# A fused attention and MLP kernel: one more batch turned by DMA, bursts keyed anew, and priorities drawn anew

## The chip, the cores and the metric

One core of one Trainium2 chip. The metric is the device time of one execution in microseconds (us), the median of several runs; lower is better.

## What is computed

Linear attention with random features, over 8 batches of 8 heads with 576 tokens each and 64 values per head, followed by an MLP over all 4608 tokens:

```python
def phi(x):
    proj = np.einsum('bhsd,md->bhsm', x, omega)
    h = proj - np.sum(x * x, axis=-1, keepdims=True) / 2.0
    h = h - np.max(h, axis=-1, keepdims=True)
    return np.exp(h) / np.sqrt(m)
kv = np.einsum('bhsm,bhsd->bhmd', k_p, v)
num = np.einsum('bhsm,bhmd->bhsd', q_p, kv)
den = np.einsum('bhsm,bhm->bhs', q_p, k_p.sum(axis=2))[..., None] + 1e-06
x = (num / den).transpose(0, 2, 1, 3).reshape(4608, 512)
h = x @ w_in                         # 512 -> 2048
g = h * np.clip(h + 3.0, 0.0, 6.0) / 6.0
out = g @ w_out                      # 2048 -> 512
```

with `q_p = phi(q * scale)` and `k_p = phi(k * scale)`.

## The kernel before

**A planner writes the order.** The kernel doesn't issue instructions as the Python runs. Each piece of work is declared with `op(engine, duration, emit, priority, reads, writes, ...)`, and `Prog.schedule` then runs a small model of the engines: it repeatedly takes, among the pieces that could start now on an engine, the one with the lowest priority value. The priorities are due times: one unit is one block of work (one batch of attention beside one block of the MLP). To them a table `NUDGE` adds some hundred small amounts, one per named piece. `Prog.emit` issues the pieces in the order found, engine by engine, with semaphores where one engine reads what another wrote. The order on each engine is fixed from then on; a piece that isn't ready holds back everything behind it on its engine, and on SP's queue every DMA behind it. PSUM is a ring of eight banks which the planner hands out.

**Attention, batch by batch** (`attention(b)`). k and q arrive from memory in bfloat16 by DMAs that GpSimd issues (from batch 1 on), v by DMAs that SP issues. 72 chunks of tokens by 64 values make 36 pairs, and two heads' chunks share a 128-row "double" (18 per batch). The steps of a batch:

- Turn k and q. For batches 0 to 2 TensorE transposes them into PSUM and DVE or ACT evacuates (`turns`); from batch 3 (`PE_T = 3`) SP issues DMA transposes.
- Project by omega. For batches 0 to 2 these are matmuls over 128 rows (pieces `K` and `Q`). From batch 3 (`ROWS = 3`) they are bursts of matmuls over 64 rows (pieces `R`, function `project_rows`, lines 736 and 739): for a range of doubles in `TU`, the two halves of the rows side by side, first all of k, then all of q. A burst takes two or four PSUM banks.
- ACT takes the exponential (pieces `eK`, `eQ`), DVE the maximum over the features (`mx`) and its reciprocal (`cc`).
- `pair(b, m)`, for each of four pairs of heads: v times the reciprocal (`vc`, on GpSimd or ACT, `vcl` on GpSimd), the product of k and v (`kv`, line 900), the numerator (`num`, line 929), the division (`div`, DVE line 945) into `xb`.
- Turn the output. For a batch below `PE_X = 3` (0, 1 and 2), `turn_x` does four TensorE transposes per pair (helper line 511) and one evacuation of 128x512 by DVE or ACT into `xT`; for the others SP issues one DMA transpose per pair (line 974). Block b of the MLP reads all of `xT` of batch b.

**MLP, block by block** (512 tokens of one batch; block 8 gathers the leftover 64 tokens of each batch). `mm1` multiplies by w_in (16 pieces of four matmuls of 512 columns, line 998), ACT takes a relu (line 1004), DVE the product with the capped half (line 1006) into `gT`. From block 1 on the second matrix product is done with seven products of quarters instead of eight (Strassen-Winograd): `products` issues pieces `P<block>.<n>` of 16 matmuls of 256 columns (line 1132), and the sums of quarters `S1` to `S4` (`combine`, line 1064, 16 per block of 128x512) run on GpSimd. Block 0 uses plain products (`mm2`, line 1048). The planner puts `products(blk - 1)` and `mm1(blk)` beside the attention of batch blk + 1.

The planner's durations that matter here:

```python
def combine(name, dst, x, y, minus, n, prio, reads, writes, engines=ADD):
    op(engines, {"POOL": 0.05 + n / 490.0, "DVE": 0.07 + n / 1920.0}, ...
```

Of the kernel before, what the change touches and what calls it, by code (L numbers as in the profile page):

```python
# [15 lines left out]
ROWS = 3  # L16
# [7 lines left out]
    ('Tevk0.11', 0): 0.0172, ('castq0.0A', 0): -0.0176, ('Tevq0.1A', 0): 0.1639, ('Tq0.1B', 0): -0.0037,  # L24
    ('Tevq0.1B', 0): 0.3021, ('Tk0.l', 0): 0.4022, ('Tevk0.l', 0): 0.0235, ('K0.0', 0): -0.1553,
    ('eK0.0', 0): -0.0153, ('K0.1', 0): 0.0442, ('eK0.1', 0): -0.0653, ('mx0.1', 0): -0.0395, ('eK0.2', 0): -0.042,
    ('K0.3', 0): 0.0766, ('K0.4', 0): 0.1229, ('eK0.4', 0): 0.2718, ('K0.5', 0): -0.0067, ('eK0.5', 0): 0.0177,
    ('K0.6', 0): -0.0736, ('eK0.6', 0): 0.1839, ('mx0.6', 0): 0.3237, ('K0.7', 0): -0.0092, ('eK0.7', 0): 0.8775,
    ('K0.8', 0): 0.0351, ('eK0.8', 0): 0.0218, ('mx0.8', 0): -0.0031, ('eQ0.0A', 1): 0.7881, ('vcl.0', 1): 0.0286,
    ('cc.0.0', 0): 0.1338, ('kvz.0.0', 0): 0.1537, ('num.0.0A', 0): 0.0042, ('rec.0.0A', 0): -0.0049,  # L30
    ('div.0.0A', 0): 0.0356, ('num.0.0B', 0): 0.0126, ('vc.0.1', 0): 0.4124, ('kv.0.1', 0): -0.0134,
    ('kvz.0.1', 0): 0.8635, ('num.0.1A', 0): 0.0126, ('rec.0.1A', 0): -0.009, ('div.0.1A', 0): 0.177,
    ('Xev.0.1A', 0): 0.6709, ('num.0.1B', 0): -0.0007, ('cc.0.2', 0): -0.0088, ('vc.0.2', 0): 0.1154,
    ('vcc.0.2', 0): -0.0808, ('num.0.2A', 0): 0.0126, ('rec.0.2A', 0): 0.08, ('vc.0.3', 0): -0.0114,
    ('vcc.0.3', 0): -0.0172, ('num.0.3A', 0): 0.7836, ('X.0.3B', 0): 0.0821, ('Xev.0.3B', 0): 0.0062,
    ('numL0', 0): -0.0033, ('divL0', 0): 0.0082, ('divL2', 0): 0.0082, ('k00.1', 0): 0.0095, ('kl.1', 0): -0.0088,
    ('ql0.1', 0): 0.0145, ('vl.1', 0): -0.119, ('v10.1', 0): -0.0099, ('Tevq1.2', 0): 0.0463, ('Tq1.4', 0): 0.7514,
    ('mx1.4', 0): -0.179, ('eK1.5', 0): 0.3592, ('mx1.5', 0): 0.3227, ('eK1.6', 0): 0.7632, ('mx1.7', 0): -0.561,
    ('mx1.8', 0): 0.0033, ('Q1.0', 1): 0.0073, ('eQ1.0', 1): 1.061, ('Q1.1', 0): 0.0184, ('Q1.1', 1): -0.0218,
    ('eQ1.1', 1): 0.9399, ('Q1.2', 1): 0.3729, ('eQ1.2', 1): -0.007, ('Q1.3', 0): 1.0729, ('vcl.1', 1): -0.0035,  # L40
    ('cc.1.0', 0): -0.1361, ('vc.1.0', 0): 0.0089, ('kv.1.0', 0): 0.0071, ('kvz.1.0', 0): -0.0003,
    ('rec.1.0A', 0): 0.0024, ('div.1.0A', 0): 0.0054, ('div.1.0B', 0): 0.0054, ('vc.1.1', 0): 0.0087,
    ('num.1.1A', 0): -0.002, ('div.1.1A', 0): 0.0054, ('div.1.1B', 0): 0.0054, ('Xev.1.1', 0): -0.0002,
    ('kv.1.2', 0): 0.9899, ('rec.1.2A', 0): -0.0101, ('div.1.2A', 0): 0.0075, ('div.1.2B', 0): 0.0054,
    ('X.1.2', 0): 0.0047, ('vc.1.3', 0): 0.6341, ('rec.1.3A', 0): -0.0016, ('div.1.3A', 0): 0.0054,
    ('div.1.3B', 0): 0.0054, ('mm1.0A.0p', 2): 0.0169, ('mm1.0A.2p', 1): 0.003, ('mm1.0A.2p', 2): 0.026,
    ('mm1.0A.4p', 2): 0.0282, ('mm1.0A.4', 0): 0.0113, ('relu.0A.4', 0): 0.1116, ('mm1.0A.6', 0): -0.0758,
    ('relu.0A.6', 0): -0.0575, ('mm1.0A.8', 0): -0.0075, ('g.0A.8', 0): -0.037, ('g.0A.10', 0): 0.0321,
    ('relu.0A.12', 0): 0.0317, ('mm1.0A.14', 0): 0.0222, ('relu.0B.12', 0): 0.7429, ('relu.0B.14', 0): 0.6881,
    ('k10.2', 0): -0.0002, ('kl.2', 0): -0.7114, ('q10.2', 0): 0.511, ('ql0.2', 0): 0.6465, ('Tevq2.3', 0): -0.6541,  # L50
    ('Tq2.4', 0): 1.2316, ('K2.2', 0): -0.7584, ('K2.5', 0): -0.3285, ('mx2.5', 0): -0.1483, ('K2.6', 0): 0.784,
    ('K2.7', 0): -0.0504, ('K2.8', 0): -0.1148, ('mm2.0.0', 3): -0.0049, ('mm2.0.0', 5): 1.9062,
    ('mm2.0.0', 6): 0.0051, ('mm2.0.1', 2): 0.0111, ('mm2.0.1', 5): 0.4836, ('mm2.0.2', 0): -0.0003,
    ('mm1.1.0', 0): -1.129, ('mm1.1.8', 0): -1.8251, ('g.1.8', 0): 0.0106, ('mm1.1.1', 0): -1.2275,
    ('mm1.1.9', 0): -0.9344, ('relu.1.9', 0): 0.0261, ('mm1.1.2', 0): -0.5674, ('mm1.1.10', 0): -1.3861,
    ('mm1.1.11', 0): -0.0435, ('mm1.1.4', 0): -0.3428, ('mm1.1.12', 0): 0.0488, ('mm1.1.13', 0): -0.1387,
    ('relu.1.13', 0): -0.4107, ('mm1.1.14', 0): 0.8048, ('mm1.1.7', 0): 0.8803, ('relu.1.7', 0): 0.0128,
    ('g.1.7', 0): -0.0389, ('mm1.1.15', 0): 1.161, ('k10.3', 0): -0.0369, ('kl.3', 0): 0.0052, ('q00.3', 0): -0.0024,
    ('q10.3', 0): 0.0694, ('ql0.3', 0): -0.0408, ('ql1.3', 0): -0.013, ('eK3.3.0', 0): 1.4387, ('R3.4', 0): -0.4628,
    ('eQ3.4', 0): -0.8607, ('kv.3.1', 0): 1.0065, ('vcc.3.2', 0): -0.4962, ('kv.3.2', 0): 0.1102,  # L60
    ('cc.3.3', 0): -0.8518, ('kvz.3.3', 0): 0.0243, ('P1.2', 0): 0.9757, ('P1.4', 0): 0.3487, ('P1.5', 1): -0.0512,
    ('P1.6', 1): 0.5369, ('mm1.2.0', 0): -1.4622, ('mm1.2.8', 0): -1.4018, ('mm1.2.1', 0): -1.442,
    ('g.2.1', 0): -0.019, ('mm1.2.9', 0): -0.3004, ('mm1.2.2', 0): -0.8136, ('mm1.2.11', 0): 0.359,
    ('mm1.2.12', 0): 0.5284, ('mm1.2.5', 0): 0.5493, ('mm1.2.6', 0): 0.5785, ('mm1.2.14', 0): 0.4337,
    ('mm1.2.7', 0): 0.6223, ('mm1.2.15', 0): 0.272, ('kl.4', 0): 1.3248, ('q00.4', 0): 3.3283, ('R4.4', 0): 1.7005,
    ('kv.4.1', 0): 1.244, ('kv.4.2', 0): 2.3155, ('rec.4.2B', 0): -0.9675, ('rec.4.3B', 0): -2.0089,
    ('P2.0', 0): 0.8372, ('mm1.3.2', 0): 0.2569, ('mm1.3.3', 0): 1.5479, ('mm1.3.4', 0): 1.276,
    ('mm1.3.5', 0): 1.2524, ('mm1.3.13', 0): 1.3245, ('mm1.3.6', 0): 1.4395, ('relu.3.6', 0): -0.4435,
    ('mm1.3.14', 0): 1.2483, ('mm1.3.7', 0): 1.5772, ('relu.3.7', 0): -0.3792, ('mm1.3.15', 0): 2.2545,
    ('kl.5', 0): 1.5071, ('q00.5', 0): -1.2639, ('eQ5.1', 0): -0.7262, ('eK5.2.0', 0): -1.0927,  # L70
    ('eK5.2.1', 0): -0.7425, ('eQ5.2', 0): -0.2778, ('eQ5.2', 1): -1.2134, ('eK5.3.0', 0): -1.1241,
    ('eQ5.3', 0): -0.7781, ('eQ5.3', 1): -1.1002, ('rec.5.0B', 0): 0.3333, ('num.5.1A', 0): 0.9799,
    ('vc.5.2', 0): -0.2083, ('div.5.2A', 0): 1.0671, ('P3.0', 0): 1.894, ('p1.3', 0): -2.2681,
    ('mm1.4.8', 0): -0.5145, ('mm1.4.1', 0): -1.527, ('S24.0', 0): 0.3404, ('relu.4.10', 0): -0.4615,
    ('mm1.4.11', 0): 0.2614, ('g.4.11', 0): 1.1488, ('S24.3', 0): -0.7607, ('eK6.0.0', 0): 1.1035,
    ('R6.1', 0): -0.8985, ('eQ6.1', 0): 1.5979, ('vc.6.0', 0): -1.609, ('vcc.6.0', 0): -1.6609, ('kv.6.0', 0): 0.7643,
    ('S44.1', 0): -1.9992, ('P4.2', 1): -0.8623, ('P4.3', 1): -2.077, ('P4.4', 1): -1.4771, ('mm1.5.0', 0): -1.6247,
    ('mm1.5.8', 0): -0.9391, ('mm1.5.1', 0): -1.9248, ('S35.0', 0): 0.1833, ('mm1.5.2', 0): -1.0023,
    ('relu.5.2', 0): 1.3127, ('mm1.5.11', 0): -1.1438, ('mm1.5.6', 0): 0.544, ('mm1.5.14', 0): 0.9483,
    ('mm1.5.7', 0): 0.6794, ('k00.7', 0): -0.8986, ('k10.7', 0): -1.1588, ('kl.7', 0): -0.7342, ('q10.7', 0): -0.2825,  # L80
    ('ql0.7', 0): -1.5109, ('ql1.7', 0): -1.5993, ('R7.1', 0): -1.3631, ('eQ7.1', 1): -0.9517, ('R7.4', 0): -0.7767,
    ('kv.7.0', 0): -0.5374, ('num.7.0A', 0): -0.5449, ('div.7.2B', 0): 1.8188, ('kv.7.3', 0): 0.8011,
    ('kvz.7.3', 0): 2.1121, ('num.7.3A', 0): 0.8703, ('P5.0', 0): 0.8394, ('P5.4', 0): 0.6698,
    ('mm1.6.0', 0): -0.9734, ('mm1.6.8', 0): -0.5602, ('mm1.6.1', 0): -0.5771, ('mm1.6.9', 0): -0.2962,
    ('mm1.6.2', 0): -0.4166, ('mm1.6.10', 0): -0.1926, ('mm1.6.3', 0): -0.3888, ('mm1.6.11', 0): 0.3862,
    ('mm1.6.12', 0): 0.4482, ('mm1.6.13', 0): 0.606, ('mm1.6.6', 0): 0.5263, ('mm1.6.14', 0): 0.7093,
    ('mm1.6.15', 0): 0.6324, ('P6.0', 0): 0.8219, ('P6.2', 0): 0.2249, ('P6.2', 1): -0.859, ('P6.4', 0): 0.6817,
    ('P6.6', 0): -0.9586, ('P6.6', 1): -1.2152, ('mm1.7.7', 0): -1.7654, ('P7.5', 1): 0.9958, ('P7.6', 1): 0.9926,
    ('mm1.8.0', 0): -0.2142, ('mm1.8.9', 0): -0.4575, ('S38.0', 0): 0.8262, ('S18.0', 0): 0.6907,
    ('mm1.8.10', 0): -0.4739, ('mm1.8.3', 0): -1.032, ('mm1.8.11', 0): -0.7425, ('S38.1', 0): -1.0861,  # L90
    ('mm1.8.4', 0): -0.632, ('mm1.8.5', 0): -0.3315, ('mm1.8.13', 0): -0.5705, ('mm1.8.7', 0): -0.5684,
# [1222 lines left out]
```

## Time and profile before

| what | us |
|---|---|
| median of 7 runs | 311.56 (310.79 to 312.59) |
| the profiled execution | 312.08 |
| its span, first to last instruction | 310.3 |
| TensorE (PE) busy in it | 300.6 |
| GpSimd (POOL) busy in it | 230.2 |
| first MLP matmul starts at | 20.27 |
| last matmul ends at | 305.21 |

The profile is of one execution; L998 is line 998 of the kernel. Of a group of instructions it tells how often they ran, the time in which at least one of them ran, the mean duration of one in nanoseconds, and how long the engine stood idle before them and what released it. Engines are PE (TensorE), PEld (its weight loads), DVE (VectorE), ACT (ScalarE), POOL (GpSimd) and SP, which only issues DMAs here. A timeline row merges neighbours of one form: start, duration of the whole row, engine, line, operation, names, shapes, count. Matmuls are pipelined, so their records overlap: a row of eight lasts seven places in the pipe and one record. A few per cent of the matmul records are missing.

### The profile page before, as it was taken

The numbers are of one execution on the slowest core, as the hardware profiler recorded it, in microseconds if no ns is written. First come the engines' busy times: TensorE is split into PE (matmuls) and PEld (weight loads), VectorE is DVE, ScalarE is ACT, GpSimd is POOL, SyncE is SP. The second block draws the span as 40 slices with busy tenths as digits, with TensorE's granted clock in tenths as the row PEclk, the third lists the DMA queues.
The fourth block names the chain that finished last, engine by engine and source line by source line (L and its number), as shares of the span: only waits on it lengthen the run. The fifth ranks groups of instructions, "written<-read, shape, count | busy, mean of one in ns | idle before, by whom it ended". The sixth has DMA issues, their size and how long they took to land.

```text
span 310.3 us, 7144 instructions
## 1 busy us (share of the span) xinstructions
PE 300.6 (97%) x2723; PEld 204.9 (66%) x2750; DVE 232.0 (75%) x511; ACT 195.4 (63%) x448; POOL 230.2 (74%) x246
## 2 busy tenths in 40 slices
PE   8999999999999999999999999998999999999993
PEld 6779956556775588556764685467756864567783
DVE  5988998698678975879687977975988637558543
ACT  3877897597658744879289737993877116455200
POOL 2777462399989797499959995999759937749990
PEclk9999999999999999999999999999999999999999
DMA  7999999796838999399949992989511201010036
GB/s 248 281 206 205 245 140 202 211 126 86 203 87 103 145 241 185 137 129 159 238 148 164 206 168 69 142 180 205 147 68 37 44 26 42 2 68 0 2 135 137
DMA packets 83218, 43.17 MB, mean 139 GB/s; under 512 B 51056, under 2 KB 80880, under 8 KB 83184
## 3 DMA queue, kind: packets, MB, share of 16 engines
q1 hardware_dynamic: 55824, 29.60, 39.8%
q0 software_dynamic: 26576, 12.46, 32.2%
q10 hardware_dynamic: 784, 0.66, 0.7%
q8 instruction: 22, 0.36, 0.5%
q14 instruction: 12, 0.10, 0.1%
HBM read 36.73 MB, written 9.44 MB: 149 GB/s over the span
## 4 chain that ended last, share of the span: by engine, by line
PE 80%; POOL 9%; ACT 3%; issue 2%; DVE 2%; DMA 2%; SPq 1%; POOLq 0%; DVEq 0%
PE p L998 31%; PE p L1132 27%; PE p L1048 5%; PE p L1023 5%; POOL s L1064 4%; PE p L929 2%; PE p L511 2%; PE p L900 2%; PE p L736 2%; DMA q<-in_q_dram 2%; POOL gT L1064 1%; POOL vc L884 1%; PE p L739 1%; PE p L771 1%; PE p L788 1%
## 5 line engine op out<-in xcount | busy, mean ns | idle before, releaser
L1006 DVE SCALAR_TENSOR_TENSOR gT<-tsb,p 128x512 f16<-128x512 f16 x128 | 84.9, 681 | 28.4 <-ACT tsb L1004 27.7
L1004 ACT ACTIVATE tsb<-p 128x512 f16<-128x512 f32 x128 | 74.7, 600 | 45.0 <-PE p L998 36.5
L998 PE MATMUL p<-xT,wi 128*128 128x512 bf16 x427 | 101.2, 379 | 1.5 <-issue 0.3
L998 PEld LDWEIGHTS p<-xT,wi 128*128 128x128 bf16 x448 | 42.2, 98 | 44.0 <-issue 1.1
L1132 PE MATMUL p<-wo,gT 128*128 128x256 f16 x368 | 45.7, 273 | 0.0
L1064 POOL TENSOR_TENSOR s<-gT 128x512 f16<-128x512 f16 x32 | 37.0, 1156 | 11.8 <-DVE gT L1006 9.8
L1064 POOL TENSOR_TENSOR s<-gT,s 128x512 f16<-128x512 f16 x32 | 37.0, 1156 | 8.8 <-DVE gT L1006 6.7
L1064 POOL TENSOR_TENSOR gT<-gT,s 128x512 f16<-128x512 f16 x32 | 36.9, 1153 | 5.7 <-PE p L1132 3.4
L1132 PEld LDWEIGHTS p<-wo,gT 128*128 128x128 f16 x368 | 35.0, 98 | 6.8 <-issue 0.8
L1064 POOL TENSOR_TENSOR gT<-gT 128x512 f16<-128x512 f16 x32 | 37.3, 1167 | 2.4
L749 ACT ACTIVATE kp<-p 128x512 bf16<-128x512 f32 (+1 forms) x50 | 25.8, 559 | 19.4 <-PE p L739 19.2
L754 DVE TENSOR_REDUCE mx<-kp 128x4 f32<-128x512 bf16 (+1 forms) x50 | 29.6, 625 | 4.5 <-ACT kp L749 4.0
L1132 PE MATMUL p<-t,gT 128*128 128x256 f16 x256 | 32.1, 273 | 0.0
L945 DVE TENSOR_TENSOR xb<-p,rec 128x384 bf16<-128x384 f32 (+1 forms) x64 | 28.5, 475 | 0.2
L884 POOL TENSOR_TENSOR vc<-v,cc 128x512 bf16<-128x512 f32 x22 | 23.4, 1062 | 6.9 <-DVE cc L878 4.9
L1132 PEld LDWEIGHTS p<-t,gT 128*128 128x128 f16 x256 | 24.2, 98 | 5.6 <-issue 1.2
L758 ACT ACTIVATE qpT<-p 128x512 bf16<-128x512 f32 (+1 forms) x50 | 26.5, 574 | 2.2 <-PE p L739 2.2
L1148 DVE TENSOR_TENSOR u<-p 128x512 f32<-128x512 f32 x16 | 11.0, 690 | 13.4 <-PE p L1132 13.4
L886 ACT ACTIVATE vc<-v,cc 128x64 bf16<-128x64 f32 x72 | 18.2, 356 | 0.0
L780 DVE TENSOR_REDUCE mx<-kp 128x4 f32<-128x512 bf16 x27 | 17.5, 674 | 0.8 <-ACT kp L777 0.7
L929 PEld LDWEIGHTS p<-kvz,qpT 128*128 128x128 bf16 x312 | 14.2, 98 | 4.9 <-ACT qpT L792 0.5
L1132 PE MATMUL p<-t,s 128*128 128x256 f16 x128 | 16.3, 273 | 0.9 <-POOL s L1064 0.8
(101 smaller groups left out, 468.3 us busy)
## 6 DMA issues: line engine op xcount, KB each, us to landing
v<-in_v_dram SPq DMA_DIRECT2D x14, 512.0 KB, 5.0
out_dram<-osb SPq DMA_DIRECT2D x14, 512.0 KB, 2.7
wi<-in_moe_w_in_dram POOLq DMA_DIRECT2D x4, 512.0 KB, 9.8
k<-in_k_dram POOLq DMA_DIRECT2D x8, 256.0 KB, 4.7
k<-in_q_dram POOLq DMA_DIRECT2D x8, 256.0 KB, 5.6
wo<-in_moe_w_out_dram POOLq DMA_DIRECT2D x8, 256.0 KB, 11.7
kb<-in_k_dram POOLq DMA_DIRECT2D x6, 256.0 KB, 4.9
qb<-in_q_dram POOLq DMA_DIRECT2D x6, 256.0 KB, 5.0
```

Of the source, the lines that this page charges most:

```text
L749: op("ACT", actt(128 * n), lambda E, lh=lh, ko=ko: E.activation(ko, out_of(0, lh).rearrange("p (x m) -> p x m", m=M), AF.Exp, scale=alpha) ...
L754: op("DVE", dvet(128 * n), lambda E, ko=ko, mo=mo: E.reduce_max(mo, ko, axis=AX.X), pos(u) + 0.03, reads=[("kp", 0, u + lh) if i else ("kp ...
L758: op("ACT", actt(128 * n), lambda E, lh=lh: E.activation(qd[:, d0:d1, lh, :], out_of(1, lh).rearrange("m (j t) -> m j t", t=128), AF.Exp, ...
L884: return E.tensor_tensor(vcm[:, :, 0:D], v32[:, m, :, :], cbc, ALU.mult)
L886: ins = E.activation(vcm[:, i, 0:D], v32[:, m, i, :], AF.Copy, scale=cc[pb][:, c0 + i:c0 + i + 1])
L929: ins = E.matmul(d[:, hh, i - i0, :], qpT[pb][:, o:o + 128], kvz[m][:, 65 * hh:65 * hh + 65], start=True, stop=True)
L945: op("DVE", dvet(128 * n), lambda E: E.tensor_tensor(xv(i0, i1), psum()[:, :, :, 0:64], rbc, ALU.mult), t + 0.01, reads=[vn, ("rec", ru)], ...
L998: ins = E.matmul(ring.t[vh.slot], wi[:, c, 128 * f:128 * f + 128], xv[:, c, :], start=(c == 0), stop=(c == NJ - 1))
L1004: op("ACT", actt(512), lambda E: E.activation(tsb[tu][:], ring.t[vh.slot], AF.Relu, bias=0.5, scale=1.0 / 6.0), t - 0.1, reads=[vh], write ...
L1006: op("DVE", dvet(512), lambda E: E.scalar_tensor_tensor(gT[gu][:, f, :], tsb[tu][:], 1.0, ring.t[vh.slot], ALU.min, ALU.mult), t - 0.1, re ...
L1064: op(engines, {"POOL": 0.05 + n / 490.0, "DVE": 0.07 + n / 1920.0}, lambda E: E.tensor_tensor(dst, x, y, ALU.subtract if minus else ALU.ad ...
L1132: ins = E.matmul(ring.t[v.slot][:, 256 * j:256 * j + 256], a[:, f, 128 * j:128 * j + 128], w[:, f, :], start=(first and f == 0 and j == 0) ...
```

## The change

It has four parts.

1. `PE_X` goes from 3 to 2, so that batch 2's output too is turned by DMA transposes from SP.
2. `project_rows` becomes `burst`, which takes a list of ranges per burst. `BURSTS` lists the same five ranges as `TU`, one to a burst. The results are named by double and half (`("kp", 0, d, lh)`) where they were named by unit, in all places that write or read them. The due times differ.
3. The planner's duration of a GpSimd sum becomes 0.07 + n/455.
4. `NUDGE` is another table.

```diff
-ROWS = 3
...
+    ROWS = 3
+    BURSTS = [[(0, 2)], [(2, 6)], [(6, 10)], [(10, 14)], [(14, 18)]]
+    RP = 1.8
...
-    PE_T, PE_X = 3, 3
+    PE_T, PE_X = 3, 2
...
-            op("PE", SWITCH + 2 * mmt(128 * n), e, pos(u) + 0.02,
...
+            p0 = (b - 1) + 0.02 + 0.075 * RP * n
+            op("PE", SWITCH + 2 * mmt(128 * total), e, p0,
...
-                   pos(u) + 0.02, reads=[bank(0, lh)[0]], writes=[("kp", 0, u + lh) if i else ("kpl", 0, lh)] + ([("kp", 0, 0)] if b == ROWS and i == 0 else []),
+                       p0, reads=[out_of_v(part, 0, lh)], writes=[("kp", 0, d, lh) for d in range(d0, d1)],
...
-                   pos(2 * i) + 0.03 + 0.045 * lh, reads=[bank(1, lh)[0]],
+                       p0 + 0.02, reads=[out_of_v(part, 1, lh)], writes=[("qpT", 0, x, lh) for x in range(d0, d1)],
...
-            for i, (d0, d1) in enumerate(TU):
-                project_rows(i, d0, d1)
+            for n, ranges in enumerate(BURSTS):
+                burst(n, ranges)
...
-        op(engines, {"POOL": 0.05 + n / 490.0, "DVE": 0.07 + n / 1920.0}, lambda E: E.tensor_tensor(
+        op(engines, {"POOL": 0.07 + n / 455.0, "DVE": 0.07 + n / 1920.0}, lambda E: E.tensor_tensor(
```

Of the two tables, entries that the text below speaks of (piece, which of that name, what is added to its priority):

```
before: ('mm1.2.0', 0): -1.4622, ('P1.2', 0): 0.9757, ('P1.4', 0): 0.3487, ('P1.6', 1): 0.5369
after:  ('mm1.2.0', 0): 0.1574, ('P1.1', 1): 2.3359, ('P1.2', 0): 0.9157, ('P1.4', 0): 2.5256, ('P1.6', 0): 1.0796,
        ('Tk2.2', 0): -1.5949, ('Tk2.3', 0): -0.2469, ('Tk2.4', 0): -0.3293, ('Tq2.l', 0): -1.9674, ('Tq2.3', 0): -0.4646,
        ('K2.1', 0): -0.5121, ('K2.2', 0): -0.4192, ('K2.3', 0): -0.3636, ('K2.4', 0): -0.3487
```

The table before had entries for pieces of blocks 7 and 8 (`mm1.7`, `P7`, `mm1.8`, `S38`, `P8`); the new one ends with block 6's products.

## The prediction

> **What bounds the kernel now.** I read the page's busy shares first, then the busy time of stretches, the chain of work that ended last, the TensorE waits, and last the timeline where TensorE stands still.
>
> The page's first part:
>
> ```profile
> PE 300.6 (97%) x2723; PEld 204.9 (66%) x2750; DVE 232.0 (75%) x511; ACT 195.4 (63%) x448; POOL 230.2 (74%) x246
> ```
>
> Busy time by stretch (columns: stretch, length, then busy time of PE, weight loads, DVE, ACT, POOL, granted clock, DMA share, GB/s):
>
> ```profile
> 0.00:20.00 20.00, 18.21 (x187) 13.49 (x188) 14.97 (x48) 13.58 (x30) 10.98 (x20) 1.00 1.03 252
> 20.00:57.00 37.00, 36.90 (x392) 28.24 (x392) 33.25 (x82) 29.48 (x73) 20.08 (x30) 1.00 1.24 211
> 57.00:91.00 34.00, 33.74 (x299) 21.97 (x303) 26.14 (x60) 24.66 (x55) 29.04 (x30) 1.00 0.76 133
> 91.00:124.00 33.00, 32.74 (x311) 22.19 (x313) 25.76 (x56) 22.07 (x53) 28.38 (x28) 1.00 0.90 158
> 124.00:240.00 116.00, 114.11 (x1061) 73.36 (x1072) 92.75 (x204) 84.63 (x205) 94.81 (x99) 1.00 0.81 147
> 240.00:305.00 65.00, 64.74 (x485) 45.64 (x488) 38.78 (x64) 20.96 (x37) 46.94 (x41) 1.00 0.15 46
> ```
>
> From 20 us on TensorE is busy almost without a break, at full clock, and the chain that ended last is TensorE for 80% of the span: the kernel is a start of 20.27 us (the first matmul of the MLP), 284.94 us of nearly gapless TensorE work to 305.21, and 5.1 us in which the last sums and stores end. Only TensorE's own work, its standstills in the middle, or the two ends can move the time. A busy PE in this profile still hides small gaps, because a matmul's record (219 ns for 128 columns) is longer than its place in the pipe; four of them take 0.39 us, so one place is (0.39 - 0.219) / 3 = 57 ns. In the same way a product matmul of 256 columns takes 109 ns (eight in 1.04 us, record 0.273), and an MLP matmul of 512 columns 216 ns.
>
> Read by starts in this way, the middle has two standstills worth naming. The larger, in the timeline:
>
> ```profile
> 212.00 1.15 POOL L1064 TENSOR_TENSOR gT<-gT 128x512 f16<-128x512 f16 x1
> ...
> 212.60 1.04 PE L1132 MATMUL p<-wo,gT 128*128 128x256 f16 x8
> ...
> 213.23 1.15 POOL L1064 TENSOR_TENSOR s<-gT,s 128x512 f16<-128x512 f16 x1
> ...
> 214.44 1.05 PE L1132 MATMUL p<-t,s 128*128 128x256 f16 x8 [0.81 <-POOL s L1064]
> 214.46 1.15 POOL L1064 TENSOR_TENSOR gT<-gT 128x512 f16<-128x512 f16 x1
> ```
>
> The group at 212.60 should give way at 212.60 + 8 x 0.109 = 213.47; the next starts at 214.44, when the sum that it reads is ready: 0.97 us lost. The sums follow one another each 1.23 us (212.00, 213.23, 214.46), although their records are 1.15. The other standstill is at 150.09, on the same kind of sum: 148.96 + 0.87 = 149.83, so 0.26 lost. Together 1.23 us.
>
> **The change part by part.**
>
> *Batch 2's output turned by transfers (PE_X 3 to 2).* It removes 4 x 4 = 16 transposes from TensorE. The row:
>
> ```profile
> L511 PE MATMUL p<-ident,xb 128*128 128x128 bf16 x48 | 5.3, 219 | 0.1
> ```
>
> 16 of these 48 are batch 2's, each 57 ns: 16 x 0.057 = 0.9 us of the bound engine. With them go four evacuations of 128x512 (0.42 us on DVE, 0.59 on ACT; both engines have 25% or more to spare, so I count nothing) and four short uses of a PSUM bank. It adds four DMA transposes on SP. They wait for the divided output, and behind them on SP's queue stand batch 3's v loads, its transposes of k and q, block 0's and 1's stores. Issue and landing of the twenty that the kernel has already:
>
> ```profile
> L974 SPq DMA_TRANSPOSE xT<-xb x20: 1190/1246/2793, 102.4 to 244.7; - x20
> ...
> DMA to landing us min/median/max: 2.4/4.2/7.1
> ```
>
> SP is not full: between 77.8 and 88.1 its issues take 0.58 + 1.27 + 0.95 + 1.64 us, so four issues of 1.25 find room there, if their order suits. DMA share is 0.76, and 4 x 128 KB are about 1% of the traffic; nothing counted.
>
> Here a rule speaks against the change. The Trainium skill, page "VectorE: DVE Perf Modes", section "The three transpose paths", gives a 128x128 bf16 transpose 390 ns on TensorE and 1309 ns by the DMA crossbar, and advises TensorE wherever PSUM will do. By its figures the edit would take 16 x 0.39 = 6.2 us off TensorE and lay 4 x 1.3 = 5.2 us of transfer on each pair of heads; by the rows it takes 0.9 us off and lays 4.2 on. The rows decide: 390 ns is near one record's length, not the price in a stream. The advice would be right if the landing were waited for. In the kernel before, the last of batch 2's output is divided at 88.09 (DVE L945, 87.20 + 0.89) and block 2's first matmul starts at 90.83, 2.74 us later. A landing 4.2 us after issue comes some 1.5 us later than that, the slowest of the twenty (7.1) some 4.4 us. The cover is block 1's products: of its 112 matmuls 72 ran before 90.83, so 40 x 0.109 = 4.4 us of them can still be put there. The new priorities do lean that way: block 1's products P1.1, P1.2, P1.4 and P1.6 get +0.9 to +2.5 (a block of work is 1.0), batch 2's turns and projections -0.2 to -2.0, and block 2's first matmul goes from -1.46 to +0.16. Bounds: 0 and +4.4 us; I take 0, as the cover equals the worst landing.
>
> *The duration of GpSimd sums.* No instruction changes, only what the planner believes: 0.05 + 512/490 = 1.095 us before, 0.07 + 512/455 = 1.195 after. The timeline says 1.23. Over the 16 sums of a block the planner was 16 x 0.135 = 2.2 us too hopeful, and will be 0.6. An order made with the smaller error should not let TensorE reach a sum 0.97 us too soon. Bounds: the 1.23 us of standstill all goes, or all stays in another place; I take that it goes.
>
> *Priorities searched anew.* A new order of thousands of places. In a queue that is gapless for 285 us a reorder can't shorten work; it can only remove or make standstills and drains. What this planner's former order left open was 1.3 us, with 0.08 us of small ones; for the new order I take half, 0.6, bounds 0 and 1.3. Start: other priorities of batch 0 may move the first MLP matmul. The chain there runs over DVE and GpSimd (vc at 13.73 takes 1.05 us), so one such step more or less on it is the bound, -0.9 to +0.9; I take 0. End: the nudges of blocks 7 and 8's last matmuls and products are gone. After the last MLP matmul its activation (0.60), product (0.68) and two sums (2.46) take 3.7 us, and five halves of the last products that need none of them take 5 x 0.87 = 4.4 us: covered; with one more sum in the queue 0.6 us would be lost. I take 0.
>
> *Bursts.* `burst` issues the same matmuls in the same ranges as `project_rows`, with the same banks. Keys by double-chunk and half say which results are read, and each reader still waits for the same evacuations. What differs is due times (0.135 apart, the q evacuations now due with the burst). A burst's price is in its neighbours:
>
> ```profile
> 90.83 4.26 PE L998 MATMUL p<-xT,wi 128*128 128x512 bf16 x19
> ...
> 95.02 0.40 PE L736 MATMUL p<-om,kT 64*128 64x128 bf16 x8
> 95.26 0.38 PE L739 MATMUL p<-qT,om 64*128 64x512 bf16 x2
> 95.57 1.05 PE L1132 MATMUL p<-wo,s 128*128 128x256 f16 x8
> ```
>
> The last 512-column matmul starts at 90.83 + 4.26 - 0.379 = 94.71 and would be through at 94.93; the burst starts at 95.02. Its own last ends 95.26 + 0.216 = 95.48, the next starts at 95.57. Each change of form costs about 0.09 us, 0.19 per stretch. The 25 bursts run in 23 stretches; two neighbours more or fewer are -0.4 or +0.4. I take 0.
>
> Sum: -0.9 (transposes) - 1.3 (standstills) + 0.6 (new ones) = -1.6 us. The profiled execution took 312.08 us for a span of 310.3, so its sum becomes 310.5 with a span of 308.7; it lay 0.52 above the median of the seven runs, 311.56. From the median: 311.56 - 1.6 = 310.0 us.
>
> **The rivals.** I count as faster or slower what differs by over 0.3% (0.93 us), about what a measurement of this kernel can tell from no change.
>
> *All goes well* (13%): no new standstill and a start shorter by 0.9: 311.56 - 0.9 - 1.3 - 0.9 = 308.5 us. For it: the start has idle TensorE. Against: nothing in the edit aims there, and one engine's nearly full queue (ACT 9.1 of 10 us from 10 to 20) limits it.
>
> *GpSimd stays late* (27%): the standstills reappear as large as before, and only the transposes are saved, some of it lost at an end: about 311.0. For it: GpSimd is full from 198 to 217 (one sum or multiply after another), and 1.195 is still under 1.23. It is "within 0.3%".
>
> *The landing is waited for* (18%, slower): block 2's first matmul waits for the last DMA transpose. Place: near 90 us. Price: up to 4.4 us with no products kept back, so -0.9 - 1.0 + 4.4 = +2.5, 314.1 us; with half of the cover there 312.5 to 313. It decides against the change once the wait is over 2.8 us (0.9 + 1.0 + 0.93), that is with fewer than 15 product matmuls left for it (4.4 - 15 x 0.109 = 2.8). For it: the slowest landing, and SP's order, in which one transpose that waits holds batch 3's transposes back too. Against: the priorities above and the spare room on SP.
>
> *It does not do what it says*: the bursts are the same work as before, which I already count at nothing.
>
> **How the numbers follow.** Likeliest case (42%): 310.0, its own range 309.3 to 310.6. Faster: 42 + 13 = 55%. Within 0.3%: 27%. Slower: 18%. The range reaches from the case in which all goes well, 308.5, to a landing partly waited for, 313.0; outside stay the worst landing and a little below.
>
> **What would show it.** Right: 32 instead of 48 xb transposes on TensorE and 24 on SP; no wait of a product for a sum near 1 us; block 2's first matmul following products without a gap; first MLP matmul near 20.3 us; 23 or so stretches of 64-row matmuls. Wrong: TensorE idle on a transpose's landing near 90 us, a sum waited for elsewhere, or a first MLP matmul that starts 0.9 us away from 20.27.

## The result, and the profile after

The changed kernel takes 309.17 us (median of 12 runs, 308.66 to 310.40) against 311.50 us: ratio 0.9925, 95% interval 0.9912 to 0.9938, a gain of 2.33 us. The forecast was 310.0 and faster, with a range of 308.5 to 313.0. The time lies in that range, but just under the range of the likeliest case, 309.3 to 310.6.

The busy shares of the kernel after are as flat as before, on a shorter span:

```profile
span 307.0 us, 7169 instructions
PE 298.5 (97%) x2710; PEld 203.6 (66%) x2737; DVE 231.1 (75%) x512; ACT 203.0 (66%) x483; POOL 225.0 (73%) x248
```

GpSimd has 5.2 us less to do, ACT 7.6 more: 120 instead of 72 of the small ACT multiplies (line 899, 886 before) that stand in for GpSimd's `vc`. The new order took this work off GpSimd; whether the longer sums or the new table led to it was not separated.

The transposes went over as the code says. The group rows of the TensorE transposes and of SP's, after:

```profile
L517 PE MATMUL p<-ident,xb 128*128 128x128 bf16 x32 | 3.7, 219 | 0.0
```

```profile
L986 SPq DMA_TRANSPOSE xT<-xb x24: 1189/1266/1988, 79.9 to 242.4; - x24
...
DMA to landing us min/median/max: 2.4/3.8/6.6
```

32 instead of 48, and 24 instead of 20. TensorE's waits in the kernel after, longest first (who waited, for whom, us in total, times, longest):

```profile
PE p L554 <- DVE fill L549: 1.3, 1, 1.3
PE p L1010 <- issue: 0.8, 5, 0.2
PE p L913 <- POOL vcl L824: 0.3, 1, 0.3
PE p L739 <- ACT qpT L766: 0.2, 1, 0.2
PE p L1144 <- POOL gT L1076: 0.2, 1, 0.2
PE p L1010 <- DVE gT L1018: 0.2, 1, 0.2
```

The first row is the very first matmul, which waits as long in the kernel before. The wait of a product for a sum that cost 0.97 us before is gone; none in the middle is over 0.4 us. The `issue` row is places of missing matmul records. No wait for a DMA is in the list.

**Where the time came from.** I subtracted from each interval between two matmul starts the first one's place in the pipe (216 ns for 512 columns, 109 for 256, 56 for 128, 31 to 33 for 65), counted a missing record as one place, and sorted the rest. The filler is matmuls on a constant, which the kernel puts between the first batch's work. Up to the start of the last matmul (304.99 us before, 302.59 after), in one execution of each kernel:

| | before | after | difference |
|---|---|---|---|
| filler and standstill before 25 us | 10.60 | 9.82 | -0.78 |
| batch 2's transposes on TensorE | 0.89 | 0 | -0.89 |
| standstills after 25 us | 1.33 | 0.98 | -0.35 |
| changes of form around the bursts (stretches) | 4.32 (23) | 3.95 (21) | -0.37 |
| sum | | | -2.39 |
| from the last matmul's start to the end | 5.28 | 4.43 | -0.85 |

The two spans differ by 3.25 us, not 2.33: the profiled execution of before took 312.08, 0.58 above its median, that of after 308.82, 0.35 below. The 0.93 of this scatter is about the size of the last row.

### The profile page after: what moved, and what is told of

It reads as the page before. It is cut to its first block, busy times and chain, and to the rows that moved or that the text cites. A ratio compares the mean times of both kernels' runs of the same rounds, so it can differ in the third digit from the quotient of the medians.

```text
span 307.0 us, 7169 instructions
## 1 busy us (share of the span) xinstructions
PE 298.5 (97%) x2710; PEld 203.6 (66%) x2737; DVE 231.1 (75%) x512; ACT 203.0 (66%) x483; POOL 225.0 (73%) x248
## 4 chain that ended last, share of the span: by engine, by line
PE 85%; POOL 3%; ACT 3%; DVE 3%; DMA 2%; issue 2%; SPq 1%; POOLq 0%
PE p L1010 32%; PE p L1144 30%; PE p L1060 5%; PE p L1035 5%; PE p L941 3%; PE p L739 2%; PE p L913 2%; PE p L517 2%; DVE gT L1018 2%; DMA q<-in_q_dram 2%; PE p L742 2%; ACT tsb L1016 1%; PE p L801 1%; PE p L782 1%; ACT vc L899 1%
## 5 line engine op out<-in xcount | busy, mean ns | idle before, releaser
L1016 ACT ACTIVATE tsb<-p 128x512 f16<-128x512 f32 x128 | 73.8, 604 | 41.3 <-PE p L1010 35.9
L899 ACT ACTIVATE vc<-v,cc 128x64 bf16<-128x64 f32 x120 | 30.3, 349 | 0.3 <-DVE cc L891 0.3
L897 POOL TENSOR_TENSOR vc<-v,cc 128x512 bf16<-128x512 f32 x15 | 16.2, 1078 | 5.0 <-DVE cc L891 3.0
L591 POOL DMA_DIRECT2D k<-in_k_dram x12 | 9.3, 777 | 13.8 <-PE p L517 9.1
```

What stands on the lines that cost most here:

```text
L899: ins = E.activation(vcm[:, i, 0:D], v32[:, m, i, :], AF.Copy, scale=cc[pb][:, c0 + i:c0 + i + 1])
L1016: op("ACT", actt(512), lambda E: E.activation(tsb[tu][:], ring.t[vh.slot], AF.Relu, bias=0.5, scale=1.0 / 6.0), t - 0.1, reads=[vh], write ...
```

## The experiments

All four take the order before, piece by piece as its planner wrote it, and change one thing in it; nothing is planned anew. (Planning anew with a table made for another kernel would change the whole order and tell nothing of one part.) In all four TensorE loses 0.19 to 0.20 us near 295 us (at 298.8 in the slowest) where the kernel before loses 0.05, and in some places several semaphores are waited for in another sequence; so they can carry a few tenths of their own. The order before was not run written out with nothing changed.

**e_turns_dma: the transfers alone.**

```diff
-PE_T, PE_X = 3, 3
+PE_T, PE_X = 3, 2
 order: X.2.m on PE, Xev.2.m on ACT or DVE
 ->     Xdma.2.m on SP, where X.2.m stood (m = 0 to 3)
```

> The order before, with batch 2's output turned by DMA transposes in the places where TensorE turned it, and nothing put in their way to cover the landing. TensorE saves 16 transposes, 0.9 us, but block 2's first matmul now waits for the last landing, 1.5 to 4.4 us later than before: with the theory that the cover by products is needed, the time is 312 to 314. Rival: the landing is hidden anyway, and the time falls by 0.9 us to 310.6.

Measured: 314.99 against 311.48 us, ratio 1.0096 (1.0070 to 1.0122): 3.0 us slower by the ratio, 3.5 by the medians, and a median above the 312 to 314 that were expected. Its timeline, SP, the last division (DVE) and TensorE:

```profile
87.03 0.89 DVE L1079 TENSOR_TENSOR xb<-p,rec 128x384 bf16<-128x384 f32 x2
...
87.95 1.17 SPq L970 DMA_TRANSPOSE xS<-xb  x1
...
89.11 1.05 PE L1266 MATMUL p<-wo,s 128*128 128x256 f16 x8
89.16 1.91 SPq L1108 DMA_TRANSPOSE xT<-xb  x1
...
92.40 1.46 PEld L1132 LDWEIGHTS p<-xT,wi 128*128 128x128 bf16 x8 [2.52 <-DMA xT<-xb]
92.63 5.95 PE L1132 MATMUL p<-xT,wi 128*128 128x512 bf16 x19 [2.47 <-DMA xT<-xb]
```

The products end at 89.11 + 8 x 0.109 = 89.98. Block 2's first recorded matmul starts at 92.63, but the record of the one ahead of it is missing (the first weights are loaded at 92.40, and the matmuls come in fours). With its place of 0.22 us put back, TensorE goes on at 92.41: 2.43 us idle, on a landing.

The transpose that it waits for was issued last, at 89.16, behind the leftover's transpose (`xS`) on SP's queue, and landed 3.2 us later. Its input had been divided at 87.03 + 0.89 = 87.92. So some 1.24 us of the wait go to the order of these two on SP, an estimate from these times, and only the rest to the missing cover; the kernel after has the leftover's transpose behind. The two were not tried apart.

The wait then costs a second time, by the clock. Busy time by stretch (columns as in the prediction; the third from the end is the clock that TensorE was granted, 1.00 being full speed):

```profile
92.40:93.70 1.30, 1.07 (x5) 0.60 (x7) 0.00 (x0) 0.22 (x1) 0.79 (x1) 1.00 0.00 0
93.70:97.10 3.40, 3.40 (x9) 1.18 (x8) 1.37 (x2) 1.67 (x4) 0.32 (x1) 0.50 0.00 0
97.10:98.50 1.40, 1.40 (x7) 0.49 (x5) 0.80 (x2) 0.61 (x2) 1.39 (x3) 1.00 0.13 14
```

TensorE is granted half of its clock for 3.4 us. The nineteen matmuls of the row at 92.63 take 5.95 us, where at one place of 0.216 each they would take 18 x 0.216 + 0.379 = 4.27: 1.68 us lost. The sum -0.89 (transposes) + 2.43 (wait) + 1.68 (clock) = +3.2 us fits the 3.0 to 3.5 measured; without the clock it would be +1.5. No other trace here has the clock under 1.00 between 20 and 300 us, nor a wait as long. The other executions of this run have no trace, but they fall in two groups: the seven with a mean granted clock of 0.995 or less took 314.43 to 315.79 us, the four with 0.997 or more 312.06 to 313.91. That the wait brought the drop is shown by its place alone.

So the slower rival of the prediction is a real mechanism. In the kernel after the same place reads:

```profile
85.26 2.59 SPq L986 DMA_TRANSPOSE xT<-xb  x2
85.37 0.89 DVE L957 TENSOR_TENSOR xb<-p,rec 128x384 bf16<-128x384 f32 x2
...
86.52 1.05 PE L1144 MATMUL p<-wo,gT 128*128 128x256 f16 x8
87.41 1.04 PE L1144 MATMUL p<-wo,s 128*128 128x256 f16 x8
...
88.92 1.05 PE L1144 MATMUL p<-wo,s 128*128 128x256 f16 x8
...
90.75 1.92 PE L1144 MATMUL p<-t,gT 128*128 128x256 f16 x16
...
93.38 4.91 PE L1010 MATMUL p<-xT,wi 128*128 128x512 bf16 x22 [0.16 <-issue]
```

The last two transposes are issued from 85.26 on. Behind them stand 40 product matmuls (4.4 us) and four bursts before the first matmul that reads their result, whose record starts at 93.38 instead of 90.83; it waits for none. (At both places the record of the first matmul is missing; it starts 0.22 us earlier.) The order makes room at the other end too: the last division ends at 86.26, where before it ended at 88.09. In this kernel the four landings took

```profile
DMA to landing us min/median/max: 3.1/5.0/6.3
```

and the last came at 92.0: its transpose was issued at 86.50 and took 5.5. About 1.2 us of the cover were to spare. Without the 40 matmuls the first reader would have come near 88.8 and waited some 3.2 us, an estimate from these times.

**e_sum: one exchange on GpSimd.**

```diff
 GpSimd, block 5:
-  S15.2 (gT<-gT)   S25.3 (s<-gT,s)
+  S25.3 (s<-gT,s)  S15.2 (gT<-gT)
```

> The order before, with one exchange on GpSimd: in block 5 the sum S2 of the last group goes ahead of the sum S1 of the group before it. If the wait of 0.97 us at 213 us is a matter of GpSimd's order, it goes and nothing takes its place: 310.5. Rival: GpSimd is full there, and the wait comes back within a few us at a product that reads the sum put later: 311.3 or more.

Measured: 310.92 us against 311.48, 0.56 less; ratio 0.9972 (0.9957 to 0.9987), which is 0.4 to 1.3 us less. Its timeline where the wait was:

```profile
210.87 2.38 POOL L1199 TENSOR_TENSOR s<-gT,s 128x512 f16<-128x512 f16 x2
...
212.69 1.04 PE L1267 MATMUL p<-wo,gT 128*128 128x256 f16 x8
213.32 2.39 POOL L1199 TENSOR_TENSOR gT<-gT 128x512 f16<-128x512 f16 x2
213.56 1.04 PE L1267 MATMUL p<-t,s 128*128 128x256 f16 x8
```

The group at 212.69 is followed at 213.56, its own eight places later; before, the next group came at 214.44. Both sums that it needs now stand in front. The 448th and the 560th recorded product matmul are 0.75 us nearer each other than before, of 0.97 us freed. So the wait was a matter of the order on GpSimd and not of too much work there, and most of it reaches the time.

**e_start: the start alone.**

```diff
 order: up to 34 us of the planner's clock
-  as before
+  as after
 order from there on, without what is done: as before
```

> The order before, written out piece by piece; only its first part, up to the point where both orders have done nearly the same work (about 34 us), is replaced by the order after. If the start is a gain of its own, TensorE's filler and standstill before 25 us falls from 10.6 us to about 9.8 and the time falls by 0.8 us, to about 310.7. Rival: the start gains nothing by itself, because what is ahead there waits later for batch 1 or the weights; then about 311.5 and a new standstill after 25 us.

Measured: 311.67 us, ratio 1.0003 (0.9992 to 1.0015): no gain. Its one trace says otherwise: the first MLP matmul at 18.82 instead of 20.27, filler and standstill before 25 us 9.85 instead of 10.60. The shift of the first matmul is more than scatter: in the three other runs, which keep the old start, it is at 20.36 to 20.55. But the last of the MLP's first 128 matmuls is at 37.71 instead of 38.27, so 0.56 is left; the splice itself loses 0.16 (at 33.8, a transpose that waits for ACT), and the last matmul starts 0.37 us earlier than before, of which the medians show nothing. Both expectations miss a part. By the interval the start is worth less than 0.3 us here, or 0.5 with the splice and the 0.14 near 295 us added. One trace of this run can't settle it.

**e_tail: one exchange on DVE at the end.**

```diff
 DVE, block 8:
-  u3.8   C11.8 (copy, then two stores)
+  C11.8  u3.8
```

> The order before, with one exchange on DVE at the very end: the copy of the finished quarter C11 of block 8 goes ahead of the sum u3, so that its two stores leave about a microsecond earlier. If the shorter tail of the kernel after (4.4 instead of 5.3 us from the start of the last matmul) comes from this, the time falls by 0.5 to 0.85 us, to about 310.8. Rival: the tail is only the scatter of one execution, and the time stays at 311.5.

Measured: 311.78 us, ratio 1.0010 (0.9991 to 1.0029): nothing. The stores did leave earlier, SP's row at the end starting at 299.82 instead of 301.30, yet its tail was 5.10 us:

```profile
299.82 7.01 SPq L1359 DMA_DIRECT2D out_dram<-osb  x6
306.93 2.10 SPq L1345 DMA_DIRECT2D out_dram<-osb  x3
```

From the last matmul's start to the end it took 5.28 us before, 5.03 in e_start, 4.64 in e_sum, 5.10 here and 4.41 in e_turns_dma. All but this one have the same order at their end, so 4.43 after is within the scatter, and the table's last row is not shown to be a gain.

## Why the prediction was right, and where its terms were off

**Transposes, -0.9: right**, by count and place: 16 x 56 ns in the table. No run turned them back on TensorE with all else as after, so their share in the 2.33 us is shown by the trace alone. One aside does not hold: 390 ns is not near one record's length, which is 219 ns here; a transpose's place in the stream is 56.

**The landing, 0: right because of the cover.** The prediction put 0 for it with bounds to +4.4, on the strength of the new priorities, and counted 40 products that could be kept back. The order after keeps back just 40, and nothing waits. e_turns_dma shows what the same edit costs in the old order: 2.43 us of wait, by the estimate above half of it from SP's order, and a time 3.0 us longer. The rival was right in mechanism and wrong in that its cover would be missing; its price, though, left out the clock, which took another 1.68 us. The advice of the Trainium skill's page "VectorE: DVE Perf Modes", section "Rules for kernel authors" (TensorE rather than the crossbar, where PSUM will do) holds in e_turns_dma, where the landing is waited for. In the kernel after, where 4.4 us of other work stand ready, no wait speaks for it; there it was not tried.

**Standstills, -1.3 + 0.6 = -0.7: mis-sized.** -0.35 came. The known 0.97 and 0.26 went. The new order left 0.98 instead of 0.6: the largest on a sum again, in block 6, where after a group of eight from 243.19 the next begins late:

```profile
243.19 1.05 PE L1144 MATMUL p<-t,s 128*128 128x256 f16 x8
244.42 1.05 PE L1144 MATMUL p<-t,gT 128*128 128x256 f16 x8 [0.18 <-POOL gT L1076]
```

243.19 + 0.87 = 244.06, so about 0.35 lost. Sums still follow one another each 1.23 us, over the 1.195 that the planner now believes. That the longer duration is what removed the wait is argued from the planner's rule; e_sum shows only that another order on GpSimd removes it.

**Start, 0 with bounds of 0.9: not foreseen, worth unsettled.** The first MLP matmul comes 1.47 us before the 20.27 of the kernel before, more than the bound, which the prediction had named as a sign of being wrong:

```profile
18.80 0.38 PE L1035 MATMUL p<-xT,wi 128*128 128x256 bf16 x2
```

In filler and standstill the table gives the start -0.78; e_start gives it at most half a microsecond.

**Bursts, 0 with bounds of 0.4: off by its own bound.** The drains cost what the prediction read (0.19 us a stretch), but the new order sets four pairs of bursts side by side where the old one set two: 21 stretches, -0.37. The prediction asked only whether the bursts do other work. Bursts apart or together, with all else equal, weren't tried.

**Sum.** -1.6 was forecast, -2.33 measured. Of the 0.73 between them +0.35 is for standstills that stayed, -0.37 for drains, and the rest, 0.7, is what the table gives to the start. As e_start doesn't confirm that, some 0.2 to 0.7 us of the gain have no shown cause. That the sum came so near is in part luck: the errors in the standstills and the drains cancel, and the start was put at nothing.

## What to carry to other kernels

When one engine is gapless, write its time as work, standstills and changes of form between its first and last instruction; an edit is worth what it takes from one of these. Moving a step to a transfer saves its time on the full engine only if the landing is covered: here the same four transposes cost 3.0 us with the order left alone and are hidden when 40 matmuls are kept back for them. Look also at what stands ahead of a transfer on its queue (1.24 us here), and at the granted clock behind a wait. A gain under a microsecond that one trace shows is not one until medians show it.

## What had not been expected

A wait of 2.43 us on TensorE was followed, 1.3 us after its end, by 3.4 us at half of the clock, which cost two thirds as much again (e_turns_dma). A single exchange of two sums on GpSimd is worth 0.6 us of 311 by the medians (e_sum), a quarter of what the whole change brought. And with one and the same order of the end, the stretch from the last matmul on took 4.4 to 5.3 us: in the kernel before one store's issue took 1.70 us where most take 0.6.
